# A three-stage attention and MoE kernel: partial outputs summed by accumulating transfers, and another order of steps in the last layer

## The chip, the core and the metric

The kernel runs on one core of one Trainium2 chip. The metric is the device time of one launch in microseconds (us). TensorE (PE) multiplies, VectorE (DVE) and ScalarE (ACT) work on vectors, GpSimd (POOL) does too and can issue transfers, and SyncE (SP) issues transfers. Each engine works through its own instructions in the order in which the program lists them, and waits on semaphores for the others.

## The reference

```python
# attention: batch 4, 8 heads, 576 tokens, head size 64, rotary positions
attn = softmax(rotate(q) @ rotate(k).T / 8) @ v
x = attn as (2304, 512)
# layer B: d_ff 1536
y = (sigmoid(x @ w_gate) * (x @ w_val)) @ w_out            # (2304, 512)
# layer C: d_ff 1024
h = y @ w_in
s = h * softmax(h)
out = (s - mean(s)) / sqrt(var(s) + 1e-6) * g_ln @ moe2_w_out   # (2304, 512)
```

## The kernel before

Every product is done with its operands split into an upper part (rounded to fp32r) and a lower part (the rest, also fp32r): upper x upper, upper x lower and lower x upper are three matmuls into the same bank. So each input needs a rounding copy (mostly ACT) and a subtraction.

The trace falls into three stretches. Attention runs to about 330 us. Layer B runs to 727.7 us: three groups of hidden columns (s = 0, 1, 2) times three blocks of 768 tokens (b = 0, 1, 2), each of about 45 us. The function `output` (from L1077) ends a half block: 48 matmuls fill the four banks a to d with the part of y that this group s contributes, four copies (ACT or DVE, L489) move them to a slot of the ring `yst` (6 slots of 384 columns), and four transfers from SP (L1105, 192 KB each) write them to memory. There are three memories `yd[s][b]`, one for each group, so the sum over s is left to layer C. In the last block (`LAST`) the tile `sg` stands in for `yst`.

Layer C works on 18 tiles of 128 tokens. For tile t:
- `load_y` (L1146) loads the three parts of y, three transfers of 256 KB; `sum_y` (L1150) adds them with two additions; `split_y` makes the upper half (ACT, L1159) and the lower half (L1161) of the sum. `y_stage` keeps three tiles of parts, two in `xst` and one in `w32`.
- H: `hidden` (L1340 to L1342), 24 matmuls of 512 columns into the bank pair `ph`, of which there are two.
- n: `normalise`, six steps: the maximum (DVE L1353), the exponential (ACT L1359), the product with its sum (DVE L1360), the square (ACT L1371, after three tiny DVE operations), a power on POOL (L1374, after two tiny DVE operations), and the scaling (DVE L1376, L1377).
- P: `pack` (L1410): upper and lower 16 bits of the result are laid side by side (one copy each on DVE and ACT), and a transposing transfer (L1395) turns them.
- u: `unpack`, four steps: the two copies back into `z` (DVE and ACT, L1410), the rounding copy (ACT L1406) and the lower half (DVE L1407).
- J: `project` (L1438 to L1440), 24 matmuls of 512 columns; then a copy (ACT L1445) and the store (L1457).

The last tile is turned on PE instead (`turn_ln`, L1427), inside J of tile 16.

Layer B and the first five tiles of layer C (up to `FIRST_C` = 5) are lists of jobs: each has an engine, a planned duration, what it reads and writes, and a time at which it is needed; `run_jobs` plays them through and fixes the order of the instructions. Jobs for `GV` go to POOL or DVE: POOL takes one only where DVE's backlog is at least `BACKLOG` = 3 us. From tile 5 on the order is written out by hand, and it is the same for every tile (one letter for each step; P is always t's own, J is tile t-5's, u is tile t-4's):

```python
do("L", t + 2); do("Y", t + 1)   # loads; two sums on POOL, upper half ACT, lower half POOL
do("H", t)
for x in 'uunununnnn': ...       # u of t-4, n of t
do("P", t)  # three times
do("J", t - AHEAD)
```

Of the kernel before, what the change touches and what calls it, by code (L numbers as in the profile page):

```python
# [14 lines left out]
ALU = mybir.AluOpType  # L15
# [5 lines left out]
def kernel(  # L21
# [322 lines left out]
    def scale_x(i):  # L344
# [5 lines left out]
    hbm = ctx.enter_context(tc.tile_pool(name="hbm", bufs=1, space=bass.MemoryType.DRAM))  # L350
    HT, BT = 384, 768
    NB = NT // BT
    xd, *yd = (
        [hbm.tile([KD * P * BT], F32, name=f"{n}{b}").rearrange("(k p t) -> k p t", k=KD, p=P) for b in range(NB)]
        for n in ("xd", "yd0_", "yd1_", "yd2_")
    )
    cd = [hbm.tile([P * 1024], F32, name=f"cd{c}").rearrange("(p a c) -> p a c", p=P, a=2) for c in range(2 * KF)]
    wd = [hbm.tile([P * 1024], F32, name=f"wd{k}").rearrange("(p c) -> p c", p=P) for k in range(4)]
# [713 lines left out]
                gate_out("d", bank["d"], pb("d"), need + 8)  # L1072
                finish("a", "5", need + 8)

    ys_used = [0]

    def output(s, b, half, setn):  # L1077

        bank, need = banks[setn], out_at(s, b, half)
        for f in range(FG):  # L1080
            where = WO_SLOTS[f]
            w = words_of(*where, 1024).rearrange("p (a c) -> p a c", a=2)
            g = gs[f, half]

            def terms(f=f, w=w, g=g):
                for m, x in enumerate("abcd"):
                    wh, wl = (w[:, a, m * P:(m + 1) * P] for a in range(2))
                    nc.tensor.matmul(bank[x], wh, g[:, 0], start=f == 0, stop=False)
                    nc.tensor.matmul(bank[x], wl, g[:, 0], start=False, stop=False)
                    nc.tensor.matmul(bank[x], wh, g[:, 1], start=False, stop=f == FG - 1)  # L1090

            at_ = one("bank", 4 * setn, 4 * setn + 4)
            reads = [words_at(where, 1024), one(f"gs{f}{half}", 0, 2)] + ([at_] if f else [])
            job(nc.tensor, 2.07, terms, reads, (at_,), need + 2 * f)
        for m, x in enumerate("abcd"):
            if (s, b) == LAST:
                t, at_ = sg[half, x], one(f"sg{half}{x}")
            else:
                k = ys_used[0] % NYS
                ys_used[0] += 1  # L1100
                t, at_ = yst[k], one("yst", k * HT, (k + 1) * HT)
            mem, mem_at = yd[s][b][m, :, half * HT:(half + 1) * HT], one(f"yd{s}_{b}", 2 * m + half, 2 * m + half + 1)
            bk = one("bank", 4 * setn + m, 4 * setn + m + 1)
            job(AV, (0.41, 0.47), lambda e, t=t, x=x: high(e, t, bank[x]), (bk,), (at_,), need + 8 + 0.2 * m)
            job(SP, 0.65, lambda t=t, mem=mem: nc.sync.dma_start(out=mem, in_=t), (at_,), (mem_at,), need + 14)  # L1105

    LAST = (NF // FG - 1, NB - 1)
    for f in range(2):
# [28 lines left out]
    YSP = 3  # L1137

    def y_stage(t):
        buf, at_ = (xst_t, 1536 * (t % 3)) if t % 3 < 2 else (w32, 0)  # L1140
        return [buf[:, at_ + 512 * s:at_ + 512 * s + 512] for s in range(3)]

    def load_y(t, s):
        b, c = divmod(t * P, BT)
        st = shaped(y_stage(t)[s], KD, P)
        nc.sync.dma_start(out=st, in_=yd[s][b][:, :, c:c + P].rearrange("k p t -> p k t"))  # L1146

    def sum_y(t, s, eng):
        st = y_stage(t)
        eng.tensor_add(out=st[0], in0=st[0], in1=st[s])  # L1150

    YSP_AT = (("xs1", 0), ("xs1", 1024), ("xs2", 0))
    LT_AT = (("xs1", 2048), ("xs2", 1024))

    def split_y(t, part=None, eng=nc.gpsimd):
        st = shaped(y_stage(t)[0], KD, P)
        ysp[t] = y = shaped(words_of(*YSP_AT[t % YSP], 1024), 2, KD, P)
        if part != 1:
            nc.scalar.copy(out=y[:, 0], in_=st)  # L1159
        if part != 0:  # L1160
            eng.tensor_sub(out=y[:, 1], in0=st, in1=y[:, 0].bitcast(F32))  # L1161

    def job_y(t, need):
        buf, at_ = ("xst", 1536 * (t % 3)) if t % 3 < 2 else ("w32", 0)
        st_at = [one(buf, at_ + 512 * s, at_ + 512 * s + 512) for s in range(3)]
        hi, lo = (words_at(YSP_AT[t % YSP], 512, 512 * a) for a in range(2))
        for s in range(3):
            job(SP, 1.0, lambda s=s: load_y(t, s), (one(f"yd{s}_0", 0, 8),), (st_at[s],), need - 8)
        for s in range(1, 3):
            job(GV, (1.33, 0.6), lambda e, s=s: sum_y(t, s, e), (st_at[0], st_at[s]), (st_at[0],), need - 4)  # L1170
        job(A, 0.52, lambda: split_y(t, 0), (st_at[0],), (hi,), need - 3)
        job(GV, (1.33, 0.6), lambda e: split_y(t, 1, e), (st_at[0], hi), (lo,), need - 2)

    def job_h(t, need):
        sets = bank_h(t)
# [63 lines left out]
    for t in range(FIRST_C):  # L1239
        job_y(t, H_AT[t])  # L1240
        job_h(t, H_AT[t])
        if t == 2:
            names = [f"gs{f}{half}" for f in range(FG) for half in range(2)]
            names += [f"sg{p_}{x}" for p_ in range(2) for x in "abcd"] + ["held1", "held5", "heldu", "held4"]
            job(V, 0.01, lambda: open_pools(), (), [one(n, 0, 2) for n in names] + [one("xs4", 0, 4 * HT), one("bank", 4, 8), one("X")], END + 9, False)
            for n in range(2):
                job_p(n, H_AT[n] + 5.5)
        job_n(t, H_AT[t] + 5.5)
        if t == FIRST_C - 1:
            job_u(0, END + 6 + 5 * t)  # L1250
        if t > 1:
            job_p(t, H_AT[t] + 5.5)
    for n in range(2):
        job_y(FIRST_C + n, END + 33 + 5 * n)
    for c in range(12, 16):
        load_unit(c, END + 15)

    def run_jobs():
# [25 lines left out]
        for _ in jobs:  # L1284
            best = None
            for e in engines:
                found = ready[id(e)]
                if e is nc.tensor:
                    found = [x for x in found if x[1] == pe[pe_at]] if pe_at < len(pe) else []
                elif e is V:  # L1290
                    own = max(free[id(e)], min((x[0] for x in found if jobs[x[1]][0] is V), default=1e9))
                    found = [x for x in found if jobs[x[1]][0] is not AV or x[0] + 1 < own or jobs[x[1]][4] < own + HURRY]
                elif e is G and found:
                    t = max(free[id(e)], min(x[0] for x in found))
                    if free[id(V)] - t + sum(took_on(x[1], V) for x in ready[id(V)] if x[0] <= t) < BACKLOG:
# [12 lines left out]
            for x in jobs[n][0] if isinstance(jobs[n][0], tuple) else (e,):  # L1308
                ready[id(x)].remove(pick)
            if e is SP:  # L1310
                bus = max(t + 1.0, bus) + took
                end[n], free[id(e)] = bus + 2.5, t + 0.42
            else:
# [162 lines left out]
    def do(kind, t):  # L1476
# [7 lines left out]
                unpacks[t] = unpack(t)  # L1484
            next(unpacks[t])
        elif kind == "Y":
            for n in range(1, 3):
                sum_y(t, n, nc.gpsimd)
            split_y(t)
        elif kind == "P":  # L1490
            if t not in packs:
                packs[t] = pack(t)
# [5 lines left out]
            project(t, 1)  # L1498
            project_out(t)
        elif kind == "L":  # L1500
            for n in range(3):
                load_y(t, n)
# [10 lines left out]
    for _, n, e in PLANNED:  # L1513
        if jobs[n][2] is not None:
            jobs[n][2](*([e] if isinstance(jobs[n][0], tuple) else []))
    for t in range(FIRST_C, NTT + AHEAD):
        if t + 2 < NTT:
            do("L", t + 2)
        if FIRST_C + 1 < t + 1 < NTT:
            do("Y", t + 1)  # L1520
        if t < NTT:
            do("H", t)
        for x in 'uunununnnn':
            if x == "n" and t < NTT:
                do("n", t)
            if x == "u" and t - LAG < NTT - 1:
                do("u", t - LAG)
        if t < NTT - 1:
            for _ in range(3):
                do("P", t)  # L1530
        do("J", t - AHEAD)
    order_ctx.close()
    c_ctx.close()

# [47 lines left out]
```

## Time and profile before

| | us |
|---|---|
| median of 3 runs | 954.95 (953.19 to 957.2) |
| the profiled execution, its own time | 956.11 |
| its span, first to last instruction | 954.3 |
| PE busy in the span | 907.7 (95%) |
| DVE, ACT, POOL busy | 790.2, 635.9, 347.0 |

In the rows, PEld is TensorE's weight load, which runs beside the matmul. A matmul's shown duration overlaps that of the next one, so the distance from one start to the next is what it costs. The span is shown in slices of 1/40 (23.86 us). In a list of waits, "A <- B: us, times, longest" says that A sat idle until B had ended. The chain of work is followed back from the last instruction to what released each step; "issue" in it is time for which the profile shows no cause.

### The profile page before, as it was taken

How to read it: one execution, taken by the hardware profiler on the slowest of the kernel's cores; microseconds unless marked ns; L12 is line 12 of the kernel's file. 1: busy time of each engine (PE TensorE's matmuls, PEld its weight loads, DVE VectorE, ACT ScalarE, POOL GpSimd, SP SyncE). 2: the span in 40 equal slices, each digit the busy share in tenths (PEclk: the TensorE clock that was granted, in tenths of full speed). 3: DMA queues.
4: the chain of work that ended last, by engine and by line, in shares of the span. 5: the costliest groups of instructions: out<-in, count | busy, mean ns of one | idle time of the engine just before them, and what ended most of it. 6: DMA issues, size and time to landing. Idle time of an engine off the chain costs nothing. (4 is left out here: it accounts for less than half of the span.)

```text
span 954.3 us, 16117 instructions
## 1 busy us (share of the span) xinstructions
PE 907.7 (95%) x5368; PEld 840.5 (88%) x5368; DVE 790.2 (83%) x1419; ACT 635.9 (67%) x1329; POOL 347.0 (36%) x284
## 2 busy tenths in 40 slices
PE   4999999999999989999999999999999989999988
PEld 4899999999989989999999999999999767777766
DVE  6999999999985898999979999988973876677761
ACT  5999999988985456575756575767652655555552
POOL 7679899898753100120201020312000123433300
PEclk9999999999999999999999999999999999999999
DMA  5668777776644752425264725366696365655522
GB/s 134 159 176 208 193 192 193 211 191 186 157 107 142 274 180 89 156 88 177 89 219 148 275 66 177 123 215 204 224 323 202 61 128 122 145 110 135 127 69 44
DMA packets 147410, 153.10 MB, mean 160 GB/s; under 512 B 55408, under 2 KB 119168, under 8 KB 147328
## 3 DMA queue, kind: packets, MB, share of 16 engines
q1 hardware_dynamic: 147328, 152.08, 55.9%
q8 instruction: 42, 0.69, 0.3%
q14 instruction: 40, 0.33, 0.1%
HBM read 84.05 MB, written 34.15 MB: 124 GB/s over the span
## 5 line engine op out<-in xcount | busy, mean ns | idle before, releaser
L304 ACT ACTIVATE e<-s,nm 128x576 f32<-128x576 f32 x144 | 107.5, 747 | 13.4 <-DVE nm L299 12.8
L299 DVE TENSOR_REDUCE nm<-s 128x1 f32<-128x576 f32 x144 | 107.2, 745 | 4.4 <-PE s L292 2.9
L375 DVE TENSOR_TENSOR et<-te,et 128x512 fp32r<-128x512 f32 x144 | 98.4, 685 | 12.4 <-ACT et L372 11.9
L292 PE MATMUL s<-st 128*128 128x288 f32 x512 | 100.5, 318 | 7.2 <-ACT e L304 5.1
L422 PE MATMUL av<-et,vs 128*128 128x288 f32 x512 | 99.9, 316 | 0.5 <-DVE uw L662 0.3
L547 POOL TENSOR_TENSOR xs<-xst,xs 128x384 fp32r<-128x384 f32 x34 | 37.9, 1140 | 160.8 <-ACT xs L543 61.0
L292 PEld LDWEIGHTS s<-st 128*128 128x128 f32 x512 | 74.5, 193 | 15.1 <-ACT e L304 10.4
L372 ACT CAST et<-te 128x512 fp32r<-128x512 f32 x144 | 84.0, 586 | 4.0 <-PE te L381 2.9
L381 PE MATMUL te<-ident,e 128*128 128x128 f32 x576 | 86.2, 273 | 0.0
L422 PEld LDWEIGHTS av<-et,vs 128*128 128x128 f32 x512 | 72.8, 189 | 3.8 <-DVE uw L662 2.5
L1374 POOL TENSOR_TENSOR st<-st,mhalf 128x1 f32<-128x1 f32 x18 | 10.0, 553 | 173.6 <-DVE st L1373 173.6
L381 PEld LDWEIGHTS te<-ident,e 128*128 128x128 f32 x576 | 70.9, 141 | 0.1
L543 ACT CAST xs<-xst 128x384 fp32r<-128x384 f32 x106 | 50.8, 516 | 13.6 <-DVE xst L538 12.5
L1407 DVE TENSOR_TENSOR xs<-z,xs 128x1024 fp32r<-128x1024 f32 x17 | 20.8, 1225 | 30.1 <-ACT xs L1406 30.1
L434 POOL TENSOR_TENSOR x_sb<-uw,um 64x576 f32<-64x576 f32 x30 | 43.6, 1454 | 3.4 <-DMA um<-uw 2.3
L169 POOL TENSOR_TENSOR turned_t<-raw_t,other_t 128x576 f32<-128x576 f32 (+1 forms) x30 | 43.7, 1479 | 1.2
L547 DVE TENSOR_TENSOR xs<-xst,xs 128x384 fp32r<-128x384 f32 x78 | 43.5, 602 | 0.0
L1340 PE MATMUL ph<-wg,xs 128*128 128x512 f32 x90 | 36.5, 406 | 6.2 <-ACT xs L1159 4.9
L1342 PE MATMUL ph<-wg,xs 128*128 128x512 f32 x90 | 37.1, 412 | 5.5 <-POOL xs L1161 5.5
L497 POOL TENSOR_TENSOR wv<-w,wv 128x768 fp32r<-128x768 f32 (+1 forms) x4 | 7.6, 1915 | 95.0 <-ACT wv L489 95.0
L466 ACT ACTIVATE mag<-raw_w 128x512 f32<-128x512 f32 x52 | 35.1, 675 | 8.1 <-DMA raw_w<-in_moe_w_val_dram 4.7
L161 POOL TENSOR_TENSOR raw_t<-raw_t,rope_sb 128x1152 f32<-128x1152 f32 x14 | 37.4, 2670 | 1.1
(358 smaller groups left out, 3059.9 us busy)
## 6 DMA issues: line engine op xcount, KB each, us to landing
st<-st SPq DMA_DIRECT2D x45, 288.0 KB
xst<-xd SPq DMA_DIRECT2D x32, 384.0 KB
yd<-yst SPq DMA_DIRECT2D x64, 192.0 KB
raw_w<-in_moe_w_out_dram SPq DMA_DIRECT2D x20, 512.0 KB
xst<-yd SPq DMA_DIRECT2D x36, 256.0 KB
st<-st SPq DMA_DIRECT2D x47, 144.0 KB
raw_w<-in_moe_w_gate_dram SPq DMA_DIRECT2D x12, 512.0 KB
raw_w<-in_moe_w_val_dram SPq DMA_DIRECT2D x12, 512.0 KB
```

What stands on the lines that cost most here:

```text
L161: eng.tensor_mul(out=(o, x)[step], in0=x, in1=w.to_broadcast([P, n, 2, D // 2]))
L169: op(out=turned[i][:, sl, hs, here].rearrange("p i h d -> p h i d"), in0=raws[i][:, hs, sl, here], in1=others[i][:, hs, sl, there],)
L292: nc.tensor.matmul(ps[:, j, :HALF], w, x, start=m == 0, stop=m == len(mm) - 1)
L299: nc.vector.tensor_reduce(out=nm, in_=ps[:, :, :HALF], axis=AX.XY, op=ALU.max, negate=True)
L304: nc.scalar.activation(out=e.rearrange("p (j c) -> p j c", j=2), in_=ps[:, :, :HALF], func=AF.Exp, bias=nm, accum_out=sums[i][:, n:n + 1],)
L372: nc.scalar.copy(out=h_out, in_=ps)
L375: nc.vector.tensor_sub(out=l_out, in0=ps, in1=h_out.bitcast(F32))
L381: nc.tensor.transpose(ps[:, r * P:(r + 1) * P], e[:, r * P:(r + 1) * P], ident)
L422: nc.tensor.matmul(av[:, :HALF], *mm[m], start=m == 0, stop=m == len(mm) - 1)
L434: eng.tensor_add(out=x_sb[hp][rows, b * S:(b + 1) * S], in0=uws.pop((i, h))[rows], in1=uws[i][rows])
L543: nc.scalar.copy(out=t[:, 0], in_=here)
L547: l_eng.tensor_sub(out=t[:, 1], in0=here, in1=t[:, 0].bitcast(F32))
```

## The change

Layer B: there is one memory `yd[b]` instead of three. Group s = 0 writes it from SP as before. Groups 1 and 2 (48 transfers of 192 KB) are issued by GpSimd and add to what lies there (`accum_op=ALU.add`). In `run_jobs` these jobs are in a set `soft`; while one is ready, GpSimd takes no other job, and each is planned with 1.3 us of GpSimd.

Layer C: a tile is one load of 256 KB, there is no `sum_y`, and there are four slots in `xst`. In the hand-written part the loads are for t+3, the halves of y for t+2 with the lower half on DVE, P is the tile before's, and the order of the steps is another one, with one form for tiles 6 to 9 and 17 (`EARLY_U`, u first), one for the other tiles, and one behind the last tile. `u_steps` hands out u of tiles 2 to 16. In the planned part u of tile 1 and the load of tile 7 are added.

```diff
-    xd, *yd = (
+    xd, yd = (
...
-            mem, mem_at = yd[s][b][m, :, half * HT:(half + 1) * HT], one(f"yd{s}_{b}", 2 * m + half, 2 * m + half + 1)
+            mem, mem_at = yd[b][m, :, half * HT:(half + 1) * HT], one(f"yd{b}", 2 * m + half, 2 * m + half + 1)
...
-            job(SP, 0.65, lambda t=t, mem=mem: nc.sync.dma_start(out=mem, in_=t), (at_,), (mem_at,), need + 14)
+            if s == 0:
+                job(SP, 0.65, lambda t=t, mem=mem: nc.sync.dma_start(out=mem, in_=t), (at_,), (mem_at,), need + 14)
+            else:
+                soft.add(len(jobs))
+                job(G, 1.3, lambda t=t, mem=mem: nc.gpsimd.dma_start(out=mem, in_=t, accum_op=ALU.add), (at_, mem_at), (mem_at,), need + 14, False)
...
-        for s in range(3):
-            job(SP, 1.0, lambda s=s: load_y(t, s), (one(f"yd{s}_0", 0, 8),), (st_at[s],), need - 8)
-        for s in range(1, 3):
-            job(GV, (1.33, 0.6), lambda e, s=s: sum_y(t, s, e), (st_at[0], st_at[s]), (st_at[0],), need - 4)
+        job(SP, 1.0, lambda: load_y(t), (one(f"yd{t * P // BT}", 0, 8),), (st_at,), need - 8)
...
-            job_u(0, END + 6 + 5 * t)
+            for n in range(2):
+                job_u(n, END + 6 + 5 * t + 4 * n)
...
+                elif e is G and any(x[1] in soft for x in found):
+                    found = [x for x in found if x[1] in soft]
...
+    EARLY_U = (6, 7, 8, 9, NTT - 1)
+    u_steps = [None] * 4
+    for t in range(2, NTT - 1):
+        u_steps += [None] * (t < 7) + [t] * 4
     for t in range(FIRST_C, NTT + AHEAD):
-        if t + 2 < NTT:
-            do("L", t + 2)
-        if FIRST_C + 1 < t + 1 < NTT:
-            do("Y", t + 1)
+        if t + 3 < NTT:
+            do("L", t + 3)
         if t < NTT:
             do("H", t)
-        for x in 'uunununnnn':
...
+        for x in "uuuuunnPPPnnYnynJ" if t in EARLY_U else "unnPPPnnYuuunynJ" if t < NTT else "uuuuJ":
+            if x == "n":
                 do("n", t)
+            elif x == "P":
+                if t > FIRST_C:
+                    do("P", t - 1)
+            elif x == "J":
+                do("J", t - AHEAD)
+            elif x in "Yy":
+                if t + 2 < NTT:
+                    split_y(t + 2, "Yy".index(x), nc.vector)
+            elif u_steps:
+                if u_steps[0] is not None:
+                    do("u", u_steps[0])
+                u_steps.pop(0)
```

## Rows read from the trace of the kernel before

**Rows 1.** The page: busy time by engine, and PEld in slices.
```profile
PE 907.7 (95%) x5368; PEld 840.5 (88%) x5368; DVE 790.2 (83%) x1419; ACT 635.9 (67%) x1329; POOL 347.0 (36%) x284
PEld 4899999999989989999999999999999767777766
```
**Rows 2.** Busy time by stretch: from:to length, PE PEld DVE ACT POOL, PEclk, DMA, GB/s.
```profile
467.00:727.70 260.70, 255.76 (x1462) 252.79 (x1461) 224.85 (x423) 160.79 (x343) 33.59 (x28) 1.00 0.59 195
727.70:762.50 34.80, 33.43 (x146) 26.84 (x145) 24.85 (x53) 19.28 (x30) 3.49 (x5) 1.00 0.38 94
762.50:910.66 148.16, 137.35 (x578) 107.69 (x576) 103.89 (x163) 81.96 (x110) 51.64 (x45) 0.99 0.56 127
910.66:949.70 39.04, 36.52 (x153) 28.49 (x151) 14.88 (x24) 16.99 (x21) 1.10 (x2) 0.96 0.24 54
```
**Rows 3.** Timeline of PE: first and last matmul of the last J (24 of them).
```profile
944.10 0.39 PE L1438 MATMUL po<-wg,xs 128*128 128x512 f32 x1
...
949.32 0.39 PE L1440 MATMUL po<-wo,xs 128*128 128x512 f32 x1
```
**Rows 4.** Waits of PE's weight loads in layer C: total us, times, longest.
```profile
PEld ph L1342 <- POOL xs L1161: 10.2, 11, 1.1
PEld ph L1340 <- ACT xs L1159: 7.6, 7, 2.9
```
**Rows 5.** Chain of work that ended last, tiles 7 and 10: start, us, what.
```profile
781.51 0.62 ACT xs L1159
...
788.90 0.56 POOL st L1374
...
794.08 0.63 ACT xs L1159
...
821.81 5.12 DMA w<-yd
```
**Rows 6.** By line: ns min/median/max; then POOL's timeline beside one of them.
```profile
L1376 DVE TENSOR_TENSOR st<-st x18: 152/161/1240, 740.7 to 921.4; 128x1 f32<-128x1 f32 x18
L1377 DVE TENSOR_SCALAR e<-e,st x16: 811/1245/1871, 754.3 to 921.6; 128x1024 f32<-128x1024 f32 x16
...
789.41 2.65 POOL L1150 TENSOR_TENSOR w<-w 128x512 f32<-128x512 f32 x2
```
**Rows 7.** Timeline of DVE, ACT and POOL: tile 17's steps, no sums beside them.
```profile
916.32 1.11 ACT L1359 ACTIVATE e<-ph,st 128x1024 f32<-128x1024 f32 x1
917.59 1.22 DVE L1360 SCALAR_TENSOR_TENSOR e<-ph,e 128x1024 f32<-128x1024 f32 x1
919.03 1.15 ACT L1371 ACTIVATE junk<-e,st 128x1024 f32<-128x1024 f32 x1 [1.52 <-DVE st L1364]
920.31 0.28 DVE L1372 TENSOR_SCALAR st<-st 128x1 f32<-128x1 f32 x1 [1.05 <-ACT junk L1371]
920.85 0.55 POOL L1374 TENSOR_TENSOR st<-st,mhalf 128x1 f32<-128x1 f32 x1 [9.39 <-DVE st L1373]
921.63 0.81 DVE L1377 TENSOR_SCALAR e<-e,st 128x1024 f32<-128x1024 f32 x1
922.36 0.74 DVE L1410 COPY z<-tp 128x1024 uint16<-128x1024 uint16 x1
923.20 1.04 ACT L1406 CAST xs<-z 128x1024 fp32r<-128x1024 f32 x1 [1.20 <-DVE z L1410]
924.27 1.22 DVE L1407 TENSOR_TENSOR xs<-z,xs 128x1024 fp32r<-128x1024 f32 x1 [1.17 <-ACT xs L1406]
925.53 0.77 DVE L1410 COPY z<-tp 128x1024 uint16<-128x1024 uint16 x1
```
**Rows 8.** Timeline of DVE: tile 5's maximum.
```profile
769.61 1.20 DVE L1353 TENSOR_REDUCE st<-ph 128x1 f32<-128x1024 f32 x1
```
**Rows 9.** Layer B, by line: SP's issues (ns min/median/max), DVE's sums (us, mean ns).
```profile
L1105 SPq DMA_DIRECT2D yd<-yst x40: 319/418/1648, 485.5 to 686.7; - x40
...
L1150 DVE TENSOR_TENSOR xst<-xst 128x512 f32<-128x512 f32 x8 | 5.3, 688 | 0.6 <-DMA xst<-yd 0.5
L547 DVE TENSOR_TENSOR xs<-xst,xs 128x384 fp32r<-128x384 f32 x48 | 27.4, 618 | 0.0
```
**Rows 10.** Timeline of ACT: first copies into the ring, two halves of a block.
```profile
675.14 0.47 ACT L489 COPY yst<-near_a 128x384 f32<-128x384 f32 x1
...
680.81 0.47 ACT L489 COPY yst<-far_a 128x384 f32<-128x384 f32 x1
```

More of the change, by code (lines that the diff above doesn't have):

```diff
@@ L352 @@
     NB = NT // BT
-    xd, *yd = (
+    xd, yd = (
         [hbm.tile([KD * P * BT], F32, name=f"{n}{b}").rearrange("(k p t) -> k p t", k=KD, p=P) for b in range(NB)]
-        for n in ("xd", "yd0_", "yd1_", "yd2_")
+        for n in ("xd", "yd")
     )
@@ L1073, in unit @@
                 finish("a", "5", need + 8)
-    ys_used = [0]
+    ys_used, soft = [0], set()
     def output(s, b, half, setn):
@@ L1139, in y_stage, with load_y @@
     def y_stage(t):
-        buf, at_ = (xst_t, 1536 * (t % 3)) if t % 3 < 2 else (w32, 0)
-        return [buf[:, at_ + 512 * s:at_ + 512 * s + 512] for s in range(3)]
-    def load_y(t, s):
+        return xst_t[:, 512 * (t % 4):512 * (t % 4) + 512]
+    def load_y(t):
         b, c = divmod(t * P, BT)
[L1145 to L1150, printed above, removed]
+        nc.sync.dma_start(out=shaped(y_stage(t), KD, P), in_=yd[b][:, :, c:c + P].rearrange("k p t -> p k t"))
     YSP_AT = (("xs1", 0), ("xs1", 1024), ("xs2", 0))
@@ L1155, in split_y @@
     def split_y(t, part=None, eng=nc.gpsimd):
-        st = shaped(y_stage(t)[0], KD, P)
+        st = shaped(y_stage(t), KD, P)
         ysp[t] = y = shaped(words_of(*YSP_AT[t % YSP], 1024), 2, KD, P)
@@ L1163, in job_y @@
     def job_y(t, need):
-        buf, at_ = ("xst", 1536 * (t % 3)) if t % 3 < 2 else ("w32", 0)
-        st_at = [one(buf, at_ + 512 * s, at_ + 512 * s + 512) for s in range(3)]
+        st_at = one("xst", 512 * (t % 4), 512 * (t % 4) + 512)
         hi, lo = (words_at(YSP_AT[t % YSP], 512, 512 * a) for a in range(2))
-        for s in range(3):
-            job(SP, 1.0, lambda s=s: load_y(t, s), (one(f"yd{s}_0", 0, 8),), (st_at[s],), need - 8)
-        for s in range(1, 3):
-            job(GV, (1.33, 0.6), lambda e, s=s: sum_y(t, s, e), (st_at[0], st_at[s]), (st_at[0],), need - 4)
-        job(A, 0.52, lambda: split_y(t, 0), (st_at[0],), (hi,), need - 3)
-        job(GV, (1.33, 0.6), lambda e: split_y(t, 1, e), (st_at[0], hi), (lo,), need - 2)
+        job(SP, 1.0, lambda: load_y(t), (one(f"yd{t * P // BT}", 0, 8),), (st_at,), need - 8)
+        job(A, 0.52, lambda: split_y(t, 0), (st_at,), (hi,), need - 3)
+        job(GV, (1.33, 0.6), lambda e: split_y(t, 1, e), (st_at, hi), (lo,), need - 2)
     def job_h(t, need):
@@ L1254 @@
         job_y(FIRST_C + n, END + 33 + 5 * n)
+    st_at = one("xst", 512 * ((FIRST_C + 2) % 4), 512 * ((FIRST_C + 2) % 4) + 512)
+    job(SP, 1.0, lambda: load_y(FIRST_C + 2), (one(f"yd{(FIRST_C + 2) * P // BT}", 0, 8),), (st_at,), END + 40)
     for c in range(12, 16):
@@ L1312, in run_jobs @@
                 end[n], free[id(e)] = bus + 2.5, t + 0.42
+            elif n in soft:
+                bus = max(t + took, bus) + 1.0
+                end[n], free[id(e)] = bus + 3.5, t + took
             else:
@@ L1486, in do @@
         elif kind == "Y":
-            for n in range(1, 3):
-                sum_y(t, n, nc.gpsimd)
-            split_y(t)
+            split_y(t, None, nc.vector)
         elif kind == "P":
@@ L1500, in do @@
         elif kind == "L":
-            for n in range(3):
-                load_y(t, n)
+            load_y(t)
         elif kind == "X":
@@ L1515 @@
             jobs[n][2](*([e] if isinstance(jobs[n][0], tuple) else []))
+    EARLY_U = (6, 7, 8, 9, NTT - 1)
+    u_steps = [None] * 4
+    for t in range(2, NTT - 1):
+        u_steps += [None] * (t < 7) + [t] * 4
     for t in range(FIRST_C, NTT + AHEAD):
-        if t + 2 < NTT:
-            do("L", t + 2)
-        if FIRST_C + 1 < t + 1 < NTT:
-            do("Y", t + 1)
+        if t + 3 < NTT:
+            do("L", t + 3)
         if t < NTT:
             do("H", t)
-        for x in 'uunununnnn':
-            if x == "n" and t < NTT:
+        for x in "uuuuunnPPPnnYnynJ" if t in EARLY_U else "unnPPPnnYuuunynJ" if t < NTT else "uuuuJ":
+            if x == "n":
                 do("n", t)
[L1526 to L1531, printed above, removed]
+            elif x == "P":
[10 more added lines that the diff above has]
+                u_steps.pop(0)
     order_ctx.close()
```

## The prediction

> **What bounds the kernel now.** I read the page first: PE is busy 95% of the span, but its weight loads, which are dense in layer B, thin out from slice 32 of 40 on, where layer C begins [rows 1]. So I went on by stretches. In layer C a matmul of 512 columns costs 5.22 us / 23 = 0.227 us from start to start [rows 3]; one H or J (24 of them) is 5.45 us, a tile 10.9 us. From 762.5 to 910.66 lie twelve H and twelve J: 130.8 us of work in 148.2 us, so PE loses 17.4 us there. The stretch before (six H, 32.7 us) loses 2.1 us, and the tail (six J and 0.8 us of transposes, 33.5 us, ending at 949.32 + 0.23) loses 5.4 us [rows 2, 3]. Together 24.9 us is all that a change of layer C can give back; its matmuls don't change.
>
> What PE waits for is seen next: the lower half of y on POOL, 10.2 us over 11 tiles, and its upper half on ACT, 7.6 us [rows 4]. The chain of work says why they are late. From one upper half to the next (781.51 to 794.08) a tile takes 12.57 us, not 10.9 [rows 5]: ACT makes the upper half of y(t+1), then unpacks tile t-4 and rounds it, DVE makes its lower half, then come product, square, power and scaling of tile t, then the pack, and only behind it in ACT's order the next upper half. Two things lengthen that chain. A tiny multiplication (L1376) takes 0.15 us alone and 1.24 us beside the first POOL sum, and the scaling (L1377) 0.81 us alone and 1.87 us beside the second: 1.09 + 1.06 = 2.15 us a tile from POOL's two sums (2.65 us) [rows 6]. And in every third tile or so the parts of y come late (a load of 5.12 us on the chain [rows 5]), as their loads stand on SP behind stores and transposes.
>
> **The change part by part, layer C.** The sums are gone, and with them the 2.15 us, POOL's 2.65 us and two loads of three. POOL keeps the power (0.55 us). The halves of y are made two tiles ahead, from a load issued three tiles ahead; H then waits for neither. The order of the steps decides the rest, so I walk it with durations that no POOL sum lengthens [rows 7]: maximum to exponential 1.25 (1.20 busy [rows 8], plus a hand-over), exponential to product 1.27, to square 1.44, to the tiny step 1.28, to the power 0.54, to the scaling 0.78, to the next DVE instruction 0.73: 7.29 us. Copy to rounding 0.84, to lower half 1.07, to what follows 1.26: 3.17 us for u. In its new place the lower half of y on DVE falls beside the power on POOL. Rows 6 show these two engines holding each other up, so I bound it by nothing and by one power, 0.55 us, and take 0.55.
>
> - Tiles 6 to 9 (u first): 7.29 + 3.17 + 0.55 = 11.0 us a tile on DVE, beside PE's 10.9. Even.
> - Tiles 10 to 16: three of the steps of u lie in the shadow of the square; on the chain stay the last lower half and n, 1.26 + 7.29 + 0.55 = 9.1 us. PE sets the pace, with 1.8 us to spare. P (0.7 us DVE, 1.05 us ACT) falls beside the exponential and the product.
>
> Is DVE in time at the start? Its maximum of tile 5 stands at 769.6 [rows 8]; I leave it there, since u of tile 1 moves ahead of it and sums move out. Then the maxima of 6 to 9 are at 780.1, 791.1, 802.1, 813.1 (7.3 + 3.2 us behind the first, then 11.0 each). On PE, J of tile 2 starts at about 784.9 and needs a lower half of 780.1; J of 3 at 795.8 needs 791.1; J of 6 at 828.5 needs 830.1 (tile 10's steps end at 813.1 + 7.9 + 7.9 = 828.9, and 1.26). H never waits: it needs the product two tiles back. So PE runs through but for about 1.3 us at tile 11. In the tail, u of tile 13 stands ahead of tile 17's maximum, and J of 14 gets its lower half some 0.8 us late.
>
> What PE still loses: 1.5 us before 762.5 (some of today's 2.1, of which part is the product of tile 2 held up by POOL), 0.6 us for J of tile 0 (u of 0 is still just ahead of it), 1.3 at tile 11, 1.1 in the tail: 4.5 us instead of 24.9, a gain of 20.4. I take 2.5 to 9 as its bounds.
>
> **Layer B.** 48 transfers leave SP (median 0.42 us, up to 1.65 to issue [rows 9]) for POOL. No row shows a transfer issued by POOL. For POOL's own time I take 1.1 us, near its smaller operations and between SP's bounds of 0.4 and 1.65: 53 us, in a stretch (467 on) where POOL is busy 33.6 of 260.7 us [rows 2]. POOL has room. Behind a waiting issue POOL queues lower halves of x and weights, which go to DVE when the planner sees a transfer ready. If all 28 POOL operations of that stretch moved, DVE had 28 x 0.62 = 17 us more, less 8 sums of 0.69 that go and three like them [rows 2, 9], so 10 us more in 36 idle us; PE would lose at most about 6 us. If few move, the sums that go are worth up to 2 us. I take a loss of 1.0. An added start-up cost of POOL's queue isn't in any row; the span and the time around it (956.1 - 954.3 = 1.8 us) bound it by 0 to some 2 us, and I take 0.
>
> **Sum.** Span 954.3 - 20.4 + 1.0 = 934.9, with 1.8 around it 936.7. The profiled execution is 1.2 us above the median, so against the runs it is 935.5; I say 936, 930 to 946 for this case.
>
> **Rivals.**
> 1. *The chain stays the pace.* If ACT's or DVE's order keeps one more hand-over on the chain than I count (the copy of the output, a pack that isn't hidden), tiles 6 to 17 take 11.7 us instead of 10.9: 12 x 0.8 = 10 us back, 946. For it: tiles 6 to 9 come out even, without slack. Against it: PE has some 5 us of lead there, and the later tiles have 1.8 us each.
> 2. *Slower: POOL's issues hold up DVE in layer B.* The place is the two-input and copy operations of DVE from 467 us on, where DVE is busy 224.9 of 260.7 us [rows 2]; the price is a DVE operation held up by a POOL one, 1.06 us [rows 6], 48 times, 51 us. DVE's idle 36 us would hide half, 18, so 33 us remain: 969. With x us for each issue the loss is 48x - 18; it passes the gain of 20 at x = 0.8. For it: rows 6. Against it: those are POOL operations that read and write 512 columns, and an issue moves no columns.
> 3. *Accumulations land late.* The ring has six slots; the third copy of a second half block needs the slot of the first copy of the half before, 5.7 us earlier [rows 10]. If POOL's issue waits behind a subtraction, or the adding transfer takes longer than about 6 us, that copy waits, and PE behind it for the bank. Ten half blocks (two for each of five blocks of s = 1 and 2 before the last), five with that reuse inside the block: 5 x 1 to 3 us, so 941 to 951.
>
> The Trainium skill speaks for rival 3 in "SBUF — State Buffer", section "SBUF: two separate sides": while a DVE instruction runs in a two-port mode, GpSimd can't write the descriptors of a transfer that it issues, and the transfer waits. The page gives 620 ns alone and 3100 ns beside such a copy; by that estimate a landing is 2.5 us later and the ring just holds. No run here shows it yet.
>
> 4. *The sums were hidden anyway.* Then 953 to 957. Rows 4 and 5 speak against it.
>
> **How the numbers follow.** Chances: the forecast 0.64, rival 1 0.13, rival 2 0.14 (0.10 of it slower, 0.04 level), rival 3 0.07, rival 4 0.02. Likeliest: 936. The range takes the forecast's bounds and the nearer rivals: 930 to 951; outside lie most of rivals 2 and 4 and a little below 930. About 0.5% is what a measurement of this kernel can tell from no change. Faster by more (under 950.2): 0.64 + 0.13 + 0.05 = 0.82. Within: 0.07 (rivals 2, 3, 4). Slower: 0.11.
>
> **What would show it.** In the profile after: weight loads by ACT's and POOL's halves of y (L1159, L1161 before) gone from PE's waits; the scaling at 0.81 us in every tile; 762.5 to the last H in about 133 us; PEld slices of layer C at 8 tenths throughout. If DVE's operations in layer B lengthen beside POOL's issues, rival 2; if ACT's copies into the ring wait for transfers, rival 3; if PE waits for L1406 or L1407 in most tiles, rival 1. The prediction is wrong if PE's gaps in layer B grow by more than 6 us, or if its loss in layer C stays above 10 us.

## The result, and the profile after

The changed kernel takes 938.62 us, the median of 4 runs (938.12 to 939.91); the kernel before, in the same sitting, 954.07 (949.76 to 957.2). The ratio is 0.9843, with a 95% interval of 0.9802 to 0.9884. The profiled execution took 939.91 us, its span is 938.1.

The page of the kernel after, PEld in slices, answers to [rows 1]:

```profile
PEld 4999999999988989999998999899999878878876
```

Behind slice 32 the weight loads now stand at 7 and 8 tenths, where [rows 1] has 6 and 7. By stretches (columns as in [rows 2]), with the boundaries at the same places of the work but for the first, 467 us, a fixed time in both: layer B, the first six H, the twelve H and twelve J behind them, the tail.

```profile
467.00:731.06 264.06, 257.98 (x1465) 252.87 (x1463) 220.46 (x415) 159.40 (x343) 71.15 (x70) 1.00 0.64 178
731.06:765.20 34.14, 33.16 (x145) 26.83 (x145) 23.80 (x51) 19.27 (x30) 6.48 (x9) 1.00 0.47 112
765.20:898.40 133.20, 131.49 (x578) 107.91 (x577) 92.57 (x178) 83.88 (x113) 12.09 (x13) 1.00 0.46 98
898.40:933.10 34.70, 34.17 (x153) 27.51 (x151) 13.12 (x20) 14.91 (x19) 0.55 (x1) 1.00 0.25 53
```

The middle of layer C went from 148.16 us [rows 2] to 133.20, beside 130.8 of work; the tail from 39.04 to 34.70. Layer B went the other way: its stretch from 467 on is 264.06 us long (x1465 matmuls recorded), before 260.70 (x1462). PE's weight loads in layer C wait for this and nothing longer (total us, times, longest), beside [rows 4]:

```profile
PEld po L1442 <- DVE xs L1409: 2.8, 3, 1.0
PEld ph L1342 <- PE ph L1344: 1.8, 2, 1.2
PEld po L1440 <- ACT xs L1408: 1.6, 2, 1.2
```

The waits for the halves of y (10.2 and 7.6 us) are gone. The granted clock of layer C was 0.99 and 0.96 in two of the stretches of [rows 2] and is 1.00 in all of them now. One tile of the kernel after, from one maximum to the next, in the timeline of DVE and POOL; L1378 and L1379 are the tiny multiplication and the scaling of [rows 6], L1159 is the lower half of y, L1376 POOL's power:

```profile
783.68 1.22 DVE L1355 TENSOR_REDUCE st<-ph 128x1 f32<-128x1024 f32 x1
...
789.41 0.69 DVE L1159 TENSOR_TENSOR xs<-xst,xs 128x512 fp32r<-128x512 f32 x1
789.51 1.00 POOL L1376 TENSOR_TENSOR st<-st,mhalf 128x1 f32<-128x1 f32 x1 [9.86 <-ACT xs L1157]
790.55 0.16 DVE L1378 TENSOR_TENSOR st<-st 128x1 f32<-128x1 f32 x1 [0.44 <-POOL st L1376]
790.74 0.81 DVE L1379 TENSOR_SCALAR e<-e,st 128x1024 f32<-128x1024 f32 x1
...
794.54 1.22 DVE L1355 TENSOR_REDUCE st<-ph 128x1 f32<-128x1024 f32 x1
```

A tile takes 794.54 - 783.68 = 10.86 us. The two steps are back at 0.16 and 0.81 us; the power takes 1.00 beside the lower half, and 0.55 without it [rows 7].

New in layer B are POOL's transfers. From the page: their queue (packets, MB, share of the 16 engines' time), their line (total us, mean ns), their issue (x40, KB, median us to landing):

```profile
q0 software_dynamic: 6912, 9.44, 6.4%
...
L1109 POOL DMA_DIRECT2D yd<-yst x40 | 36.7, 1314 | 49.3 <-ACT yst L489 47.8
...
yd<-yst POOLq DMA_DIRECT2D x40, 192.0 KB, 7.8
```

Issues that follow each other overlap in the record, so 36.7 / 40 = 0.92 us of POOL's time each.

### The profile page after: what moved, and what is told of

Read it like the earlier page. It is cut to its first block, busy times and chain, and to the rows that moved or that the text cites. A ratio compares the mean times of both kernels' runs of the same rounds, so it can differ in the third digit from the quotient of the medians.

```text
span 938.1 us, 16025 instructions
## 1 busy us (share of the span) xinstructions
PE 901.5 (96%) x5368; PEld 839.8 (90%) x5368; DVE 771.4 (82%) x1419; ACT 633.8 (68%) x1329; POOL 347.0 (37%) x296
## 3 DMA queue, kind: packets, MB, share of 16 engines
q1 hardware_dynamic: 121408, 133.20, 50.3%
q0 software_dynamic: 6912, 9.44, 6.4%
## 5 line engine op out<-in xcount | busy, mean ns | idle before, releaser
L375 DVE TENSOR_TENSOR et<-te,et 128x512 fp32r<-128x512 f32 x144 | 98.5, 685 | 12.4 <-ACT et L372 11.9
L1376 POOL TENSOR_TENSOR st<-st,mhalf 128x1 f32<-128x1 f32 x18 | 14.9, 826 | 156.4 <-ACT xs L1157 101.6
L1109 POOL DMA_DIRECT2D yd<-yst x40 | 36.7, 1314 | 49.3 <-ACT yst L489 47.8
L466 ACT ACTIVATE mag<-raw_w 128x512 f32<-128x512 f32 x52 | 35.3, 678 | 13.8 <-DMA raw_w<-in_moe_w_val_dram 6.6
L1361 ACT ACTIVATE e<-ph,st 128x1024 f32<-128x1024 f32 x16 | 17.9, 1117 | 35.9 <-DVE st L1355 35.8
L161 POOL TENSOR_TENSOR other_t<-raw_t,rope_sb 128x1152 f32<-128x1152 f32 x14 | 37.3, 2666 | 1.0
L538 DVE TENSOR_TENSOR xst<-xst 128x384 f32<-128x384 f32 x64 | 36.9, 606 | 0.3
```

The costliest lines, as they stand in the source:

```text
L161: eng.tensor_mul(out=(o, x)[step], in0=x, in1=w.to_broadcast([P, n, 2, D // 2]))
L375: nc.vector.tensor_sub(out=l_out, in0=ps, in1=h_out.bitcast(F32))
```

## The experiments

Two figures are read alike from every kernel's timeline of PE. *Idle in C*: the start of layer C's first matmul to one matmul (0.23 us) behind the start of its last, less 864 matmuls (18 H and 18 J of 24) of 0.2268 us and 0.8 us of transposes. *Way through B*: from the first matmul of `output` in group 0's second block to layer C's first matmul. It begins at 378.9 to 382.5 in all these profiles, ahead of the first adding transfer (486).

| kernel | median us | ratio to before, 95% | idle in C | way through B |
|---|---|---|---|---|
| before | 953.2 to 954.9 | | 25.05 | 345.8 |
| after | 938.62 | 0.9843 (0.9802 to 0.9884) | 5.25 | 348.9 |
| after, again (e8) | 939.35 | 0.9854 (0.9833 to 0.9875) | 5.27 | 348.0 |
| e1: adding, old order | 936.79 | 0.9833 (0.9811 to 0.9856) | 3.84 | 348.8 |
| e2: new order, POOL's sums | 954.12 | 1.0 (0.9984 to 1.0015) | 23.21 | 345.8 |
| e3: lower half of y on POOL | 942.51 | 0.9893 (0.9866 to 0.992) | 10.40 | 347.7 |
| e4: lower half of y moved | 936.25 | 0.9826 (0.9801 to 0.9852) | 4.06 | 347.5 |
| e5: ring of eight | 938.45 | 0.9838 (0.9819 to 0.9857) | 5.19 | 349.0 |
| e6: plain stores by SP | 934.82 | 0.9804 (0.9788 to 0.9819) | 5.21 | 344.8 |
| e7: plain stores by POOL | 934.86 | 0.98 (0.9781 to 0.9818) | 5.29 | 344.0 |
| e9: before, sums on DVE | 942.66 | 0.9859 (0.9823 to 0.9895) | 11.21 | 345.7 |
| e10: three buffers | 948.31 | 0.993 (0.9904 to 0.9956) | 5.26 | 359.8 |
| e11: e1, tile 7 planned | 937.51 | 0.9812 (0.9778 to 0.9846) | 3.05 | 348.6 |

### Adding without the new order (e1)

The accumulating transfers and single loads stay; layer C's steps go back to the order before, with the lower half of y on POOL.

```diff
-        for x in "uuuuunnPPPnnYnynJ" if t in EARLY_U else "unnPPPnnYuuunynJ" if t < NTT else "uuuuJ":
...
+        if FIRST_C + 1 < t + 1 < NTT:
+            do("Y", t + 1)
...
+        for x in 'uunununnnn':
...
+        if t < NTT - 1:
+            for _ in range(3):
+                do("P", t)
+        do("J", t - AHEAD)
```

> The accumulating transfers stay, so there are no sums in layer C, but the hand-written order is that of the kernel before (halves of y one tile ahead, lower half on POOL, pack behind n, u of t-4 spread between n; u of tile 1 and the load of tile 7 not in the planned part). Theory A, POOL's two sums set the pace through what they hold up on DVE: the chain of 12.57 us a tile loses 2.15 and falls to 10.4, below PE's 10.9; layer C then takes some 213 us instead of 226.6, and the time is 942 to 948. Theory B, the order sets it (the upper half of y stands at the end of ACT's chain and PE waits for it and for POOL's lower half in every tile): a tile stays over 12 us, and the time is 950 or more.

Measured: 936.79 us, level with the change or a little under it, and under the ranges of both theories. All of PE's waits in layer C, and two of DVE's maxima:

```profile
PEld ph L1339 <- PE ph L1341: 1.8, 2, 1.2
PEld ph L1341 <- POOL xs L1159: 1.1, 1, 1.1
PEld po L1439 <- DVE xs L1406: 0.9, 1, 0.9
PEld ph L1339 <- ACT xs L1157: 0.7, 1, 0.7
```

```profile
778.52 1.21 DVE L1352 TENSOR_REDUCE st<-ph 128x1 f32<-128x1024 f32 x1
...
788.98 1.22 DVE L1352 TENSOR_REDUCE st<-ph 128x1 f32<-128x1024 f32 x1
```

The old chain without sums takes 10.46 us a tile, less than PE's 10.9, so behind the waits at tile 7 PE has no further one. Theory A had the chain right (10.4) and priced it too high: layer C takes 200.6 us, not 213. Once the sums are gone, the new order adds nothing to the gain.

### The new order without adding (e2)

The counterpart: three memories, three loads and two sums on POOL stay as before, the steps stand in the new order, the lower half of y is on DVE.

```diff
+                    if x == "Y":
+                        for n in range(1, 3):
+                            sum_y(t + 2, n, nc.gpsimd)
+                    split_y(t + 2, "Yy".index(x), nc.vector)
```

> The new order alone: three memories written by SP, three loads and two POOL sums a tile, issued where the halves of y are made; lower half on DVE, as in the changed kernel. Theory A (the sums hold DVE up by 2.15 us a tile): tiles 6 to 9 take 13 us on the chain, the later ones 11.3, PE loses 8 to 12 us more than in the changed kernel, layer B starts layer C at 727.7 as before, so 943 to 948. Theory B (the order is what counts): layer C as in the changed kernel, 207 us, and the time 936 to 938.

Measured: 954.12 us, ratio 1.0: no gain at all, and above the ranges of both theories. The timeline of DVE and POOL for one tile (L1381 and L1382 are the tiny multiplication and the scaling):

```profile
810.51 1.22 DVE L1358 TENSOR_REDUCE st<-ph 128x1 f32<-128x1024 f32 x1
...
817.30 2.66 POOL L1150 TENSOR_TENSOR w<-w 128x512 f32<-128x512 f32 x2
...
817.37 1.24 DVE L1381 TENSOR_TENSOR st<-st 128x1 f32<-128x1 f32 x1 [0.44 <-POOL st L1379]
818.64 1.87 DVE L1382 TENSOR_SCALAR e<-e,st 128x1024 f32<-128x1024 f32 x1
...
823.50 1.22 DVE L1358 TENSOR_REDUCE st<-ph 128x1 f32<-128x1024 f32 x1
```

A tile takes 12.99 us here and 10.86 in the kernel after: 2.13 us more, and the two steps are longer by (1.24 - 0.16) + (1.87 - 0.81) = 2.14. From tile 8 on this costs PE some 2 us a tile and then one long wait, before J of tile 6 (PE's timeline, then the stretches of that wait and behind it, columns as in [rows 2]):

```profile
841.52 0.79 PE L1443 MATMUL po<-wg,xs 128*128 128x512 f32 x1 [6.27 <-ACT xs L1411]
...
844.62 0.79 PE L1445 MATMUL po<-wg,xs 128*128 128x512 f32 x1 [1.88 <-DVE xs L1412]
845.21 0.63 PE L1443 MATMUL po<-wv,xs 128*128 128x512 f32 x1
845.63 0.63 PE L1444 MATMUL po<-wv,xs 128*128 128x512 f32 x1
```

```profile
835.10:844.60 9.50, 1.37 (x3) 0.50 (x2) 7.74 (x14) 6.21 (x9) 3.50 (x3) 0.72 0.45 89
844.60:849.50 4.90, 4.88 (x12) 3.83 (x13) 3.97 (x8) 3.21 (x5) 0.00 (x0) 0.50 0.64 174
```

Behind 9.5 us with three matmuls the granted clock is 0.50 (1.2 GHz) for 4.9 us, and a matmul is 0.43 us from start to start instead of 0.227: twelve of them, some 2.4 us on top of the wait. The kernel before has two such stretches in layer C, which the prediction doesn't mention:

```profile
782.20:786.70 4.50, 3.87 (x10) 2.81 (x11) 2.54 (x3) 3.33 (x4) 1.28 (x1) 0.62 1.02 218
926.50:930.00 3.50, 3.50 (x11) 2.67 (x10) 1.96 (x2) 1.44 (x2) 0.00 (x0) 0.51 0.18 40
```

They follow its two longest waits (2.6 us before H of tile 7, 1.4 before J of tile 14), their matmuls are 0.43 us apart too, and together they are some 3 of its 25.05 us of idle.

With e1, this closes the square: sums gone and old order 936.8, sums gone and new order 938.6, sums kept and new order 954.1, sums kept and old order 954. That the last two agree is chance. e2 loses its time up to J of tile 6, in the form with u first and the passage to the other form. In the other form a tile with both steps held up takes 11.07 us, and from the middle of J of tile 6 to H of tile 17 PE loses 0.9 us, where the kernel before loses 6.5: there the new order does hide the sums.

### One word: the sums on DVE (e9)

How much of it is the hold-up alone? In the kernel before, the two additions go from POOL to DVE, and nothing else changes.

```diff
-                sum_y(t, n, nc.gpsimd)
+                sum_y(t, n, nc.vector)
```

> The kernel before with one edit: in the hand-written part the two sums of y run on DVE instead of POOL; three memories, three loads and the old order stay. Theory A (what counts is POOL holding DVE up, 2.15 us a tile): DVE gains 1.3 us of work in a tile but the scaling falls back to 0.81 us, the chain of a tile goes from 12.57 to about 11, layer C loses 10 to 14 us instead of 25, and the time is 940 to 946. Theory B (what counts is that the work and the two loads are gone): 951 to 956, as before or nearly.

Measured: 942.66 us, in the range of theory A; a tile takes 11.1 us, idle in C is 11.21. The timeline of DVE:

```profile
787.63 0.16 DVE L1376 TENSOR_TENSOR st<-st 128x1 f32<-128x1 f32 x1 [0.66 <-POOL st L1374]
787.83 0.81 DVE L1377 TENSOR_SCALAR e<-e,st 128x1024 f32<-128x1024 f32 x1
...
789.28 1.41 DVE L1150 TENSOR_TENSOR w<-w 128x512 f32<-128x512 f32 x2
```

The two sums take DVE 1.41 us, less than the 2.15 us by which it was held up when POOL made them in 2.65. So 25.05 - 11.21 = 13.8 of the 19.8 us that layer C gave back come from taking them off POOL, some 3 of them as the clock stays at 1.00 (2.4 GHz). The rest (6 us to the change, 7.4 to e1) lies with DVE's 1.41 us and the two further loads of a tile; these two weren't separated.

### The lower half of y (e3, e4)

e3: the lower half of y goes back to POOL, in the new order.

```diff
-                    split_y(t + 2, "Yy".index(x), nc.vector)
+                    split_y(t + 2, "Yy".index(x), nc.gpsimd)
```

> The changed kernel with the lower half of y on POOL in the hand-written part. Theory A (what POOL holds up counts): the subtraction, 1.29 us on POOL, stands behind the power and beside DVE's scaling, which it holds up by some 1.1 us; tiles 6 to 9 take 11.6 us on DVE's chain instead of 11.0, the wait before the J of tile 11 grows by 2 us or more: 940 to 943. Theory B (DVE's load counts): DVE is 0.69 us lighter in every tile, 936 to 938.

Measured: 942.51 us, 3 to 4 above the change; idle in C 10.40. The timelines of POOL and DVE:

```profile
786.58 1.29 POOL L1159 TENSOR_TENSOR xs<-xst,xs 128x512 fp32r<-128x512 f32 x1
```

```profile
780.30 1.22 DVE L1355 TENSOR_REDUCE st<-ph 128x1 f32<-128x1024 f32 x1
...
786.64 1.25 DVE L1378 TENSOR_TENSOR st<-st 128x1 f32<-128x1 f32 x1 [0.66 <-POOL st L1376]
...
791.73 1.22 DVE L1355 TENSOR_REDUCE st<-ph 128x1 f32<-128x1024 f32 x1
```

The subtraction on POOL starts 0.06 us ahead of the tiny multiplication and holds it for its own length: 1.25 us instead of 0.16, and a tile of 11.43, as theory A has it. Of the 5.2 us that this adds to the idle, some 2 are the clock: behind a wait of 3.6 us before J of tile 6 it is 0.50 from 832.0 to 836.6 us. So the move to DVE is right in the new order. In the old one (e1) the same subtraction on POOL does no harm.

e4: for tiles 6 to 9 the lower half of y moves from beside the power into DVE's wait for ACT inside u.

```diff
-        for x in "uuuuunnPPPnnYnynJ" if t in EARLY_U else "unnPPPnnYuuunynJ" if t < NTT else "uuuuJ":
+        for x in "uuzuuunnPPPnnYnnJ" if t in EARLY_U else "zunnPPPnnYuuunynJ" if t == 10 else "unnPPPnnYuuunynJ" if t < NTT else "uuuuJ":
...
+            elif x == "z":
+                if 7 < t + 1 < NTT and t < 11:
+                    split_y(t + 1, 1, nc.vector)
```

> The changed kernel with the lower half of y, in tiles 6 to 9, moved away from POOL's power to where DVE waits for the rounding copy of u (for the next tile; tile 10 makes one left over). Theory A (the power and the subtraction hold each other up, 0.45 us a tile, and these add up to the 1.8 us that PE waits at 831 us): that wait shrinks to 0.5 us or goes, 936.5 to 938. Rival: the wait comes from where DVE stands at tile 5; it stays, 938 to 940.

Measured: 936.25 us, idle in C 4.06. DVE's timeline:

```profile
790.21 1.22 DVE L1355 TENSOR_REDUCE st<-ph 128x1 f32<-128x1024 f32 x1
...
798.18 0.69 DVE L1159 TENSOR_TENSOR xs<-xst,xs 128x512 fp32r<-128x512 f32 x1
...
800.62 1.22 DVE L1355 TENSOR_REDUCE st<-ph 128x1 f32<-128x1024 f32 x1
```

A tile is 10.41 instead of 10.86 us, so the 0.45 us by which the lower half lengthened the power did lie on the chain. PE's wait at tile 11 falls from 1.8 to 0.6 us, and no more is to be had, since PE is the pace. The time itself can't be told from the change's.

### Layer B: the ring, the issue, or the adding (e5, e6, e7, e8)

e5: two more slots for the copies, so that none waits for a transfer.

```diff
-    NYS = 6
+    NYS = 8
```

> The changed kernel with 8 slots in the ring instead of 6, so that no copy out of the banks waits for a transfer of the half block just before it. Theory A (the 3 us by which layer C starts later than before come from copies that wait for accumulating transfers, median 7.8 us from issue to landing): layer C starts 1.5 to 3 us earlier than in the changed kernel (731.1), at 728 to 729.6, time 936 to 938. Theory B (they come from POOL's subtractions that the planner gave to DVE): layer C starts at 731 as in the changed kernel.

Measured: 938.45 us. In the kernel after, ACT's waits in layer B have this row, which e5 hasn't:

```profile
ACT yst L489 <- DMA yd<-yst: 3.7, 2, 2.0
```

Rival 3's wait was thus there, in two places; without it the way through B is 349.0 us, as long as with it. ACT's next wait, for a weight store (`cd`), takes 3.6 us instead of 3.2 there, so what the ring gives back is waited for a little later.

e6 and e7: groups 1 and 2 of layer B are stored plainly into memories that nobody reads (their share is left out of the output), from SP in e6, from POOL in e7. Layer C is that of the change. Of e7:

```diff
-                job(G, 1.3, lambda t=t, mem=mem: nc.gpsimd.dma_start(out=mem, in_=t, accum_op=ALU.add), (at_, mem_at), (mem_at,), need + 14, False)
+                other = yx[s - 1][b][m, :, half * HT:(half + 1) * HT]
+                job(G, 1.3, lambda t=t, other=other: nc.gpsimd.dma_start(out=other, in_=t), (at_, mem_at), (mem_at,), need + 14, False)
```

> The changed kernel with groups 1 and 2 written by SP, without adding, to memories that nothing reads; the output leaves these two groups out. What the whole path through POOL costs layer B: with it gone layer C starts at 727.7 plus or minus 1 by theory A (waits for transfers) and by theory B (moved subtractions). If it starts at 731 too, neither is the cause and it is the order that the planner finds once the sums are gone.

> As the last, but groups 1 and 2 are issued by POOL, without adding, to memories that nothing reads; the output leaves these two groups out. If it is the adding that makes a transfer land late (7.8 us): landing falls to 3 to 5 us, no copy waits for the ring, layer C starts at 728 to 729.5. If it is the way through POOL's queue: landing stays at 6 to 9 us and layer C starts at 731.

> The changed kernel once more, on the chip of the three runs above, so that 2 us can be told: layer C starts at 730.5 to 731.5, time 938 to 940.

Measured in one sitting: 934.82 (SP), 934.86 (POOL), and 939.35 for the change itself (e8). The engine that issues makes no difference to the sum (e6's plan of layer B is another order of steps, so this compares two plans); the adding costs 4.5 us. All of it lies in layer B. PE's timeline has the two ends of the way, first for the kernel after, then for e7:

```profile
382.20 0.33 PE L1088 MATMUL near_a<-gs,wo 128*128 128x384 f32 x1
...
731.06 0.39 PE L1342 MATMUL ph<-wg,xs 128*128 128x512 f32 x1
```

```profile
382.48 0.33 PE L1089 MATMUL near_a<-gs,wo 128*128 128x384 f32 x1
...
726.52 0.39 PE L1344 MATMUL ph<-wg,xs 128*128 128x512 f32 x1
```

In the table the seven kernels that add (e10 aside) need 347.5 to 349.0 us for it, the five others 344.0 to 345.8. The same bytes from POOL without adding, on e7's page (queue, line, issue):

```profile
q0 software_dynamic: 3072, 9.44, 2.6%
...
L1111 POOL DMA_DIRECT2D yx<-yst x40 | 22.0, 554 | 57.2 <-ACT yst L490 55.0
...
yx<-yst POOLq DMA_DIRECT2D x40, 192.0 KB, 5.3
```

Where it bites shows in other waits: in the kernel after, engines that prepare weights wait for the weight stores `cd` to land before they overwrite a buffer. DVE's waits in layer B, after and then e7:

```profile
DVE rawv L469 <- DMA cd<-rawv: 5.1, 3, 2.6
```

```profile
DVE rawv L470 <- DMA cd<-rawv: 1.3, 1, 1.3
```

ACT has 3.2 us of the same kind in the kernel after and 0.8 in e7; the list of before has none.

These two profiles can be laid over each other. Behind 331 us the 911 recorded operations of DVE, the 681 of ACT and the 105 of POOL come in the same order in both, so each start has its counterpart. PE falls 4.8 us behind e7 between 497 and 692 us: 0.6 at 497, 1.3 at 506, 0.8 at 598 and 609, 1.1 at 655 to 658, 0.5 at 676, 0.4 at 691. The largest step, in the timelines of ACT and PE of the kernel after, then of ACT in e7:

```profile
504.95 0.69 ACT L466 ACTIVATE mag<-raw_w 128x512 f32<-128x512 f32 x1 [3.23 <-DMA cd<-mag]
506.06 0.45 PE L723 MATMUL far_c<-xs,wv 128*128 128x384 f32 x1 [1.14 <-ACT held L1015]
```

```profile
502.21 0.68 ACT L467 ACTIVATE mag<-raw_w 128x512 f32<-128x512 f32 x1 [0.83 <-DMA cd<-mag]
```

ACT waits 3.23 instead of 0.83 us for a weight store out of `mag`; its next operation is the copy `held` that frees the bank `far_c`, and PE waits 1.14 us for that, where e7's PE has no wait (504.41). The step at 497 stands behind ACT's two waits for the ring (1.97 and 1.75 us, 0.15 and 0.28 in e7); those at 598 and 609 behind loads of weights that land late (4.0 us of waits on DVE and ACT, none in e7); those from 655 to 691 behind DVE's waits for `cd` (1.86 us at 650 and 0.62 at 688, none in e7). e8 laid over e7 shows 3.9 us, most of it at the same places. So the additions cost time where transfers land late, and that is mostly not their own landing but that of the stores and loads of weights beside them.

### Three buffers for the weights (e10)

If those waits are the cost, a third buffer of each kind should give it back. (A small tile was moved to make room.)

```diff
-    vals = [t[:, :512] for t in rawv]
+    vals = [t[:, :512] for t in rawv] + [b_left.tile([P, 512], F32, name="val2")]
+    mags.append(b_left.tile([P, 512], F32, name="mag2"))
...
-        k = raws_used[0] % 2
+        k, j = raws_used[0] % 2, raws_used[0] % 3
```

> The changed kernel with three buffers in place of two for the decoded weights of layer C and their upper halves, which layer B stores while the adding transfers run. Theory A (the adding transfers make those stores land late, and ACT and DVE wait for the two buffers, some 9 us in all, against 2 us where POOL's transfers don't add): these waits fall under 3 us, and the way from block (0,1) to layer C shortens from 348 to 349 us to 345 to 346.5; time 935.5 to 937.5. Rival (these waits have slack, the loss comes from elsewhere): the way stays at 348 to 349, time 938 to 940.

Measured: 948.31 us, far above both ranges; layer C is unchanged, the way through B 359.8. The planner found another order, in which the weights themselves come late. DVE's waits in layer B:

```profile
DVE w L469 <- DMA raw_w<-in_moe_w_val_dram: 9.5, 3, 5.0
```

This says nothing for or against the buffers: the edit moved the whole plan. It shows that a plan of layer B can differ by 11 us through what looks like more room.

### The old order with tile 7 ahead (e11)

e1's one wait was at tile 7; here its load and halves go into the planned part.

```diff
-    for n in range(2):
+    for n in range(3):
         job_y(FIRST_C + n, END + 33 + 5 * n)
```

> The first experiment (accumulating transfers, old order) with the load and the halves of y of tile 7 in the planned part, so that PE needn't wait for them after tile 6. If the wait before tile 7's H is all that the old order still loses against an unbroken PE, layer C's loss falls from 3.8 to 2.5 us, time 934.5 to 936.5; if DVE's and ACT's chain, 10.4 us a tile by the first estimate, isn't in time after all, the wait comes back some tiles later and the time is that of the first experiment, 936 to 938.

Measured: 937.51 us, idle in C 3.05, the lowest of all but not the 2.5 of the forecast: the wait moved to tile 8 and shrank to 0.7 us. The 0.8 us against e1 are seen in the profile and can't be seen in the time, which lies in the range that was given for no gain.

## Why the prediction was right, and where not

The forecast was 936 us with 930 to 951 around it; 938.6 was measured. Its sum, step by step, against the profiled execution:

| term | forecast | measured |
|---|---|---|
| what a tile of 6 to 9 takes on DVE | 11.0 | 10.86 |
| the lower half of y beside the power | 0.55 (0 to 0.55) | 0.45 |
| PE's loss before J of tile 0 | 1.5 | 1.5 |
| at J of tile 0 | 0.6 | 0.7 |
| at tile 11 | 1.3 | 1.8 |
| in the tail | 1.1 | 1.1 |
| gain of layer C | 20.4 | 25.05 - 5.25 = 19.8 |
| loss of layer B | 1.0 (-2 to 6) | 348.9 - 345.8 = 3.1 |
| span | 934.9 | 938.1 |

The measured terms sum to 937.6; of the 0.5 us that are left, half lie ahead of the way through B and half behind layer C.

**Layer C was right in its size and in its places.** The hold-up of DVE by POOL's sums, 2.15 us out of [rows 6], is 2.14 in e2. As a price for every tile of the kernel before it is too high: [rows 6] give maxima, and the median of the tiny step is 0.161 us. Beside the sums of the hand-written part, made for eleven tiles, the tiny step is long six times and the scaling eight times, together 14.6 us, so 1.3 a tile. And the prediction put all of the 24.9 us down to waits, where some 3 are matmuls at 1.2 GHz behind the longest two of them; they went with these waits. The signs that were named came too: the waits for L1159 and L1161 are gone from PE's list, the scaling takes 0.811 to 0.815 us in all 16 tiles, the middle stretch is 133.2 us for "about 133". Of PEld's slices in layer C some stay at 7 tenths where 8 were said. (The losses in the table sum to 5.1; the idle of 5.25 also holds what the rounding and the mean of 0.2268 us leave over.)

**Its reason was half wrong.** After the sums the prediction says "the order of the steps decides the rest". It doesn't. The numbers to see this stood in it: 12.57 us of chain a tile [rows 5] less 2.15 is 10.42, below PE's 10.9; e1 measured 10.46. (Both steps were held up in the tile of [rows 5], so the subtraction holds for it.) With the sums gone the old order was already fast enough, and walking through the new one priced something with no effect. e2 shows the other half: with the sums there, the new order, with halves made two tiles ahead, gives nothing back on the whole; what its later tiles win, its earlier ones lose. The parts of y that came late "in every third tile or so" needed no earlier issue either: with one load instead of three, e1 waits for halves of y in one tile only (0.7 and 1.1 us).

**Layer B is the term that was mis-sized**, by 2.1 us in this profile (e8: 348.0, so 1.2). The prediction looked for the cost in POOL's queue and in DVE's load. POOL's issue was rightly sized (0.92 us for the 1.1 taken), and few POOL operations moved: of the 70 in the stretch 45 are issues, so 25 are left of 28, while DVE got 4 us less to do. The step that failed is that the forecast priced layer B by POOL and DVE alone: the cost is the addition in the transfer, 4.5 us between e7 and e8, through other transfers that land late. Against before it is less, as what the change takes out of layer B's stretch gave 1 to 2 us back (344.0 and 344.8 in e7 and e6, 345.8 before, in single profiles).

**The rivals.** Rival 1, the chain stays the pace (946): no; 10.86 against 10.9 was enough, and e4's 10.41 bought nothing that the time shows. Rival 2, POOL's issues hold up DVE (969): no. Of DVE's operations between 325 and 760 us, 76 lay beside issues alone and were together 0.1 us longer than the median of their kind; 96 lay beside other POOL operations and were 14.2 us longer. That was the reason given against it, that an issue moves no columns. Rival 3, late landings (941 to 951): the condition came true, 7.8 us against the 6 that decided, and two copies waited 3.7 us, but in one half block only and not in five, and PE fell 0.6 us behind; e5, without these waits, gains nothing. So the price was wrong, and the late landings that cost were those of other transfers. Rival 4: no.

The rule of the Trainium skill that was weighed for rival 3 ("SBUF — State Buffer", section "SBUF: two separate sides") made a landing 2.5 us later where DVE copies; no run here took DVE's copies away, so none shows it. What the runs do separate is the addition: 7.8 us against 5.3, with 6912 packets for 3072 and 6.4% of the engines' time for 2.6%, at the same 9.44 MB. The Trainium skill has a reason that may hold here in "Collectives: The Full Stack", section "The bandwidth ceiling: the fold count and why AG ≠ RS ≠ AR": the adding step of a collective reads two sources, with a descriptor for each, and so comes out at half the rate of a copying one. The factors of 2.25 and 2.5 here are near that; that a kernel's adding transfer works like a collective's step no run here shows.

**What stays open.** Why the stores and loads of weights land later while additions are under way: the order of the operations is the same in e7, the addition and the memory that is written differ, and how the one delays the other isn't seen. Nor whether more buffers would give the time back: e10, made for that, changed the plan as a whole. Nor is there a version that is surely faster than the change: e1, e4 and e11 lie 1 to 2.5 us below it, and their intervals overlap with its own.

## What to carry to other kernels

Before an order of steps is rebuilt, subtract: chain of one round less the hold-up that the other part of the change removes, held against the bound engine's time; if that is already below, the reordering has little left to win. Take the hold-up from the same round, not from the longest that a list shows. Where a change has several parts, run the square of them (each alone, both, none); two kernels told here what no reading of the changed trace could. Where two kernels run the same operations in the same order, lay their profiles over each other and look at where the distance grows. Work moved from an engine into a transfer is not free: 48 adding transfers cost 4.5 us here, in a stretch where POOL had room and the issues held up no one; what paid were engines that waited for other transfers.

## What the runs showed of the hardware

- An adding transfer of 192 KB by GpSimd landed after 7.8 us (median, 3.7 to 12.4), a plain one of the same size, issued at the same place in the order, after 5.3. It made 2.25 times the packets, and its issue cost POOL 0.92 us instead of 22.0 / 40 = 0.55. Other transfers landed later beside such ones: DVE and ACT waited 8.3 us for stores of weights and 4.0 us for loads, with plain transfers in the same order 2.1 us and none.
- A POOL operation on 512 columns holds up even a DVE multiplication of a single column, for nearly its own length: 0.16 to 1.24 us behind an addition, 1.25 behind a subtraction. POOL's issues of transfers don't (0.1 us over 76 operations). The Trainium skill has the first in "SBUF — State Buffer", section "Who interferes with whom": two inputs from SBUF meet GpSimd's reads, and the later one waits for the whole instruction.
- After 9.5 us with three matmuls the granted clock stood at 0.50 (1.2 GHz) for 4.9 us of full work (e2), which cost PE about 2.4 us on top of the wait. It also fell behind a wait of 3.6 us (e3, 0.50 for 4.6 us) and, in the kernel before, behind waits of 2.6 and 1.4 us (0.62 for 4.5 us, 0.51 for 3.5 us).
